# New priority keys for the list scheduler of an attention + gated-MLP kernel

## The chip, the cores and the metric

One core of a Trainium2 chip runs the whole kernel. The metric is device time in microseconds (us), the median of several executions.

## The reference, cut to what matters

```python
# B, H, S, D = 8, 12, 448, 64 ; float32 throughout
scores = cap * tanh((q @ k.T / 8) / cap)
attn   = exp(scores - max(scores)); attn /= sum(attn) + 1e-9
x      = heads_side_by_side(attn @ v)              # (8, 448, 768)
h      = relu(x @ w_in); u, w = h[..., :512], h[..., 512:]
w      = (w - mean(w)) / sqrt(var(w) + 1e-6)       # over the 512 features
gated  = u * (w_spatial @ w + b_spatial)           # mixes the 448 positions
out    = gated @ w_out                             # (8, 448, 768)
```

## The kernel before, in words

The Python code first lists every piece of work as a task (engine, modelled duration, a priority number called its key, the tasks it depends on, the buffers it takes). `Plan.order` then plays the engines forward in time with the modelled durations. Whenever an engine is free, it takes the task with the smallest key among those that are ready and whose buffers are free. The order that comes out is the order of the instructions on each engine's queue, and it is fixed: on the chip each queue runs in that order and waits for what it needs. Two rules matter beside the keys. A buffer of a kind is handed out strictly in the order of the keys of the tasks that ask for one, even when a later one is ready first. And TensorE (PE), which works either in the 64x64 tiles of the attention (mode "R") or with the whole 128x128 array (mode "N"), adds `STICK` to the key of a task that would change the mode.

**Attention** is done in 24 quads, three per batch; a quad (`quad_bnd`, number `turn`) is 4 heads. It loads the raw q and k of two head pairs (`raw`, 4 buffers) and v (`v`, 2 buffers: one quad's worth). Seven score groups of 8 matmuls (L594, `sc`) go to PSUM. ScalarE (ACT) takes the tanh of each (L598) into `tp` (6 buffers of two groups; a quad needs 4) and the exp of each pair (L605). Seven groups of 8 matmuls multiply by v (L615, `pv`). VectorE (DVE) folds the exps over keys to a maximum (`mx`), then to a sum (`sm`): six instructions each, L633 four times, L641, L643, in the single `red` buffer. For the quads 0 to 2 the sum is done on PE instead (L662, in the two `acc` PSUM buffers, brought out by ACT at L671). Small instructions make the denominators (`dn`, L652 to L685), which go through memory and come back spread over partitions (L686, L689). DVE multiplies (L698), and each head pair is cast (ACT, L355) and split (DVE, L351) into a high and a low part in an `xg` buffer (7 of them), the input of the MLP.

**The MLP** of a batch (`moe`) needs its three quads, as six `xg` chunks, and consists of 18 units on PE, each a chain of matmuls into one `acc` buffer: u (L754 to L756, 4 units of 18 matmuls), v (L776 to L781, 4 units, 66 matmuls in all), g (L845 to L850, 4 units of 11) and o (L870 to L872, 6 units of 12), 254 matmuls. In batch 0 the u units 0 and 1 come first, with 8 filler matmuls ahead (L753); in the others the four v units.

**The weights** arrive as 64-bit numbers: 12 pieces of w_in (`wi`), 12 of w_out (`wo`, through `xg` buffers), 4 of w_spatial (`ws`). A piece of `wi` or `wo` takes one POOL (GpSimd) instruction (L420), three on DVE (L424, L425, L427), a cast (ACT, L355) and a DVE subtraction (L351); `ws` has its subtraction on POOL.

The keys are sums: for stage `s` of quad `t`, index `i`, `4*t + BND_KEY[s] + BND_ADJ[s or "sc", t] + BND_KEY[s_]*i`; for unit `n` of batch `b`, `12*(b+1) + BND_KEY["moe"] + BND_ADJ["moe"b] + n*(span + span_b)/18`; the MLP's DVE and ACT tasks add `mv`; the weights have `BND_W_KEYS` and the `wi`, `ws`, `wo` entries.

Of the kernel before, what the change touches and what calls it, by code (L numbers as in the profile page):

```python
# [42 lines left out]
class Plan:  # L43
# [5 lines left out]
    SEM = {"T": 230.0, "V": 200.0, "A": 200.0, "P": 230.0, "S": 0.0}  # L49
    SAME = {"T": 0.0, "A": 60.0, "V": 60.0, "P": 60.0, "S": 0.0}  # L50
    HAND, WINDOW = 70.0, 4096 / 1.2
    TURN, STICK = 180.0, 5.6142

    OWN = {"vtr", "red3", "max", "stat", "gmul", "vadd", "xadd", "rec", "ones", "evl", "evh", "nb"}

# [160 lines left out]
def gpc(n):  # L216
# [26 lines left out]
CAP_BITS = 0x42200000  # L243
ANY_KEY = dict(moe=0.5, span=12.0, mv=0.0)
ANY_W_KEYS = 2, 0.5, 8, 9, 1, 5, 0.5
BND_KEY = dict(ld=20.2062, vld=16.3748, sc=-4.4101, th=2.6266, ex=-12.5751, pv=3.8334, sm=4.9568, mx=1.2536,
               dn=-1.9573, ev=0.5509, x=0.5743, moe=3.5126, span=11.5964, step=-1.1271, mv=-7.699, vld_=0.5863, sc_=0.1716,
               th_=0.234, ex_=3.1048, pv_=-0.3915, sm_=-0.1418, mx_=1.5249)
BND_ADJ = dict(sc0=-1.9208, sc1=-0.6751, sc2=-0.5665, sc3=0.6591, sc4=1.0022, sc5=0.9243, sc6=0.5641, sc7=3.5286,
               sc8=4.1291, sc9=2.1364, sc10=0.4432, sc11=-0.3562, sc21=1.0782, sc22=-2.0787, sc23=-1.8651, mx0=7.5468, mx1=4.1712,  # L250
               mx2=0.2306, mx3=-3.4986, mx4=-4.2501, mx5=-7.8699, mx6=-6.59, mx7=-4.2274, mx8=-1.6152, mx9=-1.0965, mx10=-2.503,
               mx11=2.4712, mx21=3.6487, mx22=7.5152, mx23=10.1101, sm0=-23.9232, sm1=-5.9121, sm2=-19.3382, sm3=-4.1068,
               sm4=-7.6692, sm5=-6.9113, sm6=-7.6076, sm7=-2.9296, sm8=-4.8786, sm9=-2.9017, sm10=0.1476, sm11=-1.028,
               sm21=7.8004, sm22=5.003, sm23=9.0892, dn0=-13.9326, dn1=2.5665, dn2=1.5054, dn3=3.678, dn4=5.4586, dn5=2.0101,
               dn6=-0.9345, dn7=1.341, dn8=5.2032, dn9=5.9753, dn10=6.5428, dn11=-0.3824, dn21=0.2627, dn22=-7.9155, dn23=32.9005,
               x0=-1.8155, x1=-12.9607, x2=-3.0392, x3=-3.3476, x4=1.7459, x5=0.4945, x6=3.9029, x7=6.1809, x8=0.3782, x9=6.0115,
               x10=5.0057, x11=0.7894, x21=7.5672, x22=-1.7504, x23=1.6104, moe0=-2.1731, moe1=4.7513, moe2=2.8101, moe3=2.4916,
               moe7=9.0071, span0=-2.667, span1=-3.3859, span2=-2.449, span3=-5.6885, span7=28.8127, mv0=4.9503, mv1=-2.4788,
               mv2=2.6326, mv3=3.2084, mv7=-12.8989, wi0=-3.2806, wi1=-21.6066, wi2=-37.6263, wi3=14.5167, wi4=16.5614,
               wi5=1.1376, wi6=13.0344, wi7=2.468, wi8=-18.9783, wi9=3.3202, wi10=-13.2504, wi11=-12.154, ws0=-12.654,  # L260
               ws1=-7.9959, ws2=-33.2129, ws3=-10.2049, wo0=-6.4452, wo1=-0.8201, wo2=2.6051, wo3=8.6589)
BND_V_FIRST = 1
WARM, WARM_N, FILL = 14, 512, 8
BND_W_KEYS = -14.6272, 0.1578, -3.1507, 14.803, -4.1788, 0.5729, 0.2535
SPARE = ()
PE_SUMS = 3
E_W = "PAV"
# [6 lines left out]
def attn_moe(ctx, tc, bounded, shared, qk, v, qk2, v2, cap, w_in, w_sp, w_out, out):  # L274
    nc = tc.nc
    TAGS, PTAGS = (BND_TAGS, BND_PTAGS) if bounded else (ANY_TAGS, ANY_PTAGS)
    KEY, W_KEYS, V_FIRST = (BND_KEY, BND_W_KEYS, BND_V_FIRST) if bounded else (ANY_KEY, ANY_W_KEYS, B)
    PS = bass.MemoryType.PSUM
# [159 lines left out]

    adj = lambda name, i: BND_ADJ.get(name + str(i), 0.0) if bounded else 0.0
    wi32, wo32 = w_in.bitcast(U32), w_out.bitcast(U32)  # L440
# [124 lines left out]
    def quad_bnd(b, n):  # L565

        at, turn = b * H + 4 * n, b * (NP // 2) + n
        own_key = lambda name: KEY[name] + BND_ADJ.get((name if name in ("mx", "sm", "dn", "x") else "sc") + str(turn), 0.0)
        kk = lambda name, i=0: at + own_key(name) + KEY.get(name + "_", KEY["step"]) * i
# [161 lines left out]
    def moe(b, xs):  # L731
        own_key = lambda name: KEY[name] + (BND_ADJ.get(name + str(b), 0.0) if bounded else 0.0)
        k0 = (b + 1) * H + own_key("moe")
# [221 lines left out]
```

## Time and profile before

| | |
|---|---|
| median of 3 runs | 729.02 us (728.62 to 729.78) |
| profiled execution, first to last instruction | 726.5 us |
| around the span (difference to the median) | 2.5 us |
| busy in the span | PE 713.2, DVE 600.4, ACT 479.9, POOL 78.4 us |
| matmuls | 4910 |
| granted TensorE clock, mean | 0.997 |

The profiled execution has no other time of its own than its span; the runs' median stands 2.5 us above it. Busy shares are averages over stages with different limits; a busy PE can still lose time between matmuls, since their ends are modelled.

### The profile page before, as it was taken

The numbers are of one execution on the slowest core, as the hardware profiler recorded it, in microseconds if no ns is written. First come the engines' busy times: TensorE is split into PE (matmuls) and PEld (weight loads), VectorE is DVE, ScalarE is ACT, GpSimd is POOL, SyncE is SP. The second block draws the span as 40 slices with busy tenths as digits, with TensorE's granted clock in tenths as the row PEclk, the third lists the DMA queues.
The fourth block names the chain that finished last, engine by engine and source line by source line (L and its number), as shares of the span: only waits on it lengthen the run. The fifth ranks groups of instructions, "written<-read, shape, count | busy, mean of one in ns | idle before, by whom it ended". The sixth has DMA issues, their size and how long they took to land.

```text
span 726.5 us, 12274 instructions
## 1 busy us (share of the span) xinstructions
PE 713.2 (98%) x4910; PEld 487.7 (67%) x4910; DVE 600.4 (83%) x849; ACT 479.9 (66%) x648; POOL 78.4 (11%) x71
## 2 busy tenths in 40 slices
PE   8998999999999999999999999999999999999997
PEld 3333576575668657785568688568566865699896
DVE  4899999999999989948999996299799778983520
ACT  6999757849883894649875833786876678424321
POOL 1234310600110001000120001000021000200100
PEclk9999999999999999999999999999999999999999
DMA  8564314524221431033321430124321131202002
GB/s 279 165 204 148 129 38 134 168 80 142 85 78 30 149 129 49 28 91 114 102 76 28 153 103 27 49 66 141 102 77 41 47 131 39 53 2 101 1 1 80
DMA packets 34263, 66.50 MB, mean 92 GB/s; under 512 B 6034, under 2 KB 21908, under 8 KB 34196
## 3 DMA queue, kind: packets, MB, share of 16 engines
q1 hardware_dynamic: 34196, 65.62, 28.3%
q8 instruction: 40, 0.66, 0.4%
q14 instruction: 27, 0.22, 0.1%
HBM read 54.40 MB, written 11.18 MB: 90 GB/s over the span
## 4 chain that ended last, share of the span: by engine, by line
PE 79%; DVE 12%; issue 4%; ACT 2%; DMA 1%; SPq 1%; POOL 0%; DVEq 0%; ACTq 0%; POOLq 0%
PE ps_s L594 13%; PE ps_x L615 13%; PE ps_acc L870 5%; PE ps_acc L871 5%; PE ps_acc L872 5%; PE ps_acc L754 4%; PE ps_acc L756 4%; PE ps_acc L755 4%; DVE red L633 4%; PE ps_acc L779 4%; PE ps_acc L780 3%; PE ps_acc L781 3%; PE ps_acc L848 2%; PE ps_acc L850 2%; PE ps_acc L849 2%
## 5 line engine op out<-in xcount | busy, mean ns | idle before, releaser
L598 ACT ACTIVATE tp<-ps_s,capt 128x896 f32<-128x896 f32 x168 | 162.2, 1003 | 28.6 <-PE ps_s L594 18.1
L633 DVE TENSOR_TENSOR red<-red,tp 128x1792 f32<-128x1792 f32 x90 | 140.9, 1566 | 22.5 <-ACT tp L605 20.8
L605 ACT ACTIVATE tp<-tp,capt 128x1792 f32<-128x1792 f32 (+1 forms) x96 | 154.0, 1606 | 1.5
L594 PE MATMUL ps_s<-raw 64*64 64x448 f32 x1344 | 147.1, 545 | 3.6 <-ACT tp L598 3.5
L615 PE MATMUL ps_x<-tp,v 64*64 64x448 f32 x1344 | 140.0, 536 | 0.5 <-ACT tp L605 0.4
L633 DVE TENSOR_TENSOR red<-tp 128x1792 f32<-128x1792 f32 x45 | 91.2, 2027 | 13.9 <-ACT tp L605 13.0
L615 PEld LDWEIGHTS ps_x<-tp,v 64*64 64x64 f32 x1344 | 51.3, 133 | 75.7 <-issue 68.2
L594 PEld LDWEIGHTS ps_s<-raw 64*64 64x64 f32 x1344 | 47.1, 132 | 80.1 <-issue 46.5
L803 POOL TENSOR_TENSOR lst<-lst,capt 128x1 f32<-128x1 f32 x32 | 34.9, 1091 | 526.7 <-DVE lst L801 482.9
L754 PE MATMUL ps_acc<-xg,wi_h 128*128 128x448 f32 x180 | 66.2, 368 | 0.5 <-ACT xg L355 0.5
L755 PE MATMUL ps_acc<-xg,wi_h 128*128 128x448 f32 x180 | 65.3, 363 | 0.7 <-DVE xg L351 0.6
L756 PE MATMUL ps_acc<-xg,wi_l 128*128 128x448 f32 x180 | 65.2, 362 | 0.0
L870 PE MATMUL ps_acc<-xg,wo_h 128*128 128x448 f32 x176 | 64.5, 367 | 0.0
L871 PE MATMUL ps_acc<-xg,wo_h 128*128 128x448 f32 x176 | 63.7, 362 | 0.6 <-DVE xg L351 0.6
L872 PE MATMUL ps_acc<-xg,wo_l 128*128 128x448 f32 x176 | 63.8, 362 | 0.0
L355 ACT CAST xg<-o 128x448 fp32r<-128x448 f32 x32 | 18.1, 566 | 55.0 <-DVE o L855 49.5
L641 DVE STREAM_TRANSPOSE red<-red 128x896 f32<-128x896 f32 x45 | 49.6, 1102 | 0.7
L779 PE MATMUL ps_acc<-wi_h,xg 128*128 128x512 f32 x126 | 50.1, 398 | 0.0
L643 DVE TENSOR_REDUCE st<-red 128x28 f32<-128x896 f32 x45 | 48.6, 1079 | 0.7
L780 PE MATMUL ps_acc<-wi_l,xg 128*128 128x512 f32 x126 | 49.1, 390 | 0.0
L781 PE MATMUL ps_acc<-wi_h,xg 128*128 128x512 f32 x126 | 49.1, 390 | 0.0
L633 DVE TENSOR_TENSOR red<-red 128x896 f32<-128x896 f32 x45 | 48.6, 1079 | 0.6
(146 smaller groups left out, 1110.1 us busy)
## 6 DMA issues: line engine op xcount, KB each, us to landing
raw<-in_qk SPq DMA_DIRECT2D x48, 448.0 KB
rr<-rd SPq DMA_DIRECT2D x48, 224.0 KB
out<-o SPq DMA_DIRECT2D x48, 224.0 KB
w<-in_w_in SPq DMA_DIRECT2D x12, 512.0 KB
v<-in_v SPq DMA_DIRECT2D x24, 256.0 KB
v<-in_v SPq DMA_DIRECT2D x24, 192.0 KB
xg<-in_w_out SPq DMA_DIRECT2D x12, 256.0 KB
rd<-dt SPq DMA_DIRECT2D x48, 3.5 KB
```

What stands on the lines that cost most here:

```text
L594: nc.tensor.matmul(ps.t[c * D:(c + 1) * D, e, :S], lhsT=f(raw[c].t)[r, k:k + D], rhs=f(raw[c].t)[r, :S], start=True, stop=True)
L598: th = add("A", act(PW, 1), kk("th", i), lambda ps=ps, tp=tp, o=o: nc.scalar.activation(out=tp.t[:, o:o + PW].rearrange("p (e q) -> p e q" ...
L605: ex = add("A", act_s(w, 1), kk("ex", i), lambda tp=tp, w=w: nc.scalar.activation(out=tp.t[:, :w], in_=tp.t[:, :w], func=AF.Exp, scale=ca) ...
L615: nc.tensor.matmul(x.t[e * D:(e + 1) * D, c, :S], lhsT=vts[g // 2].t[c * D:(c + 1) * D, (4 * (g % 2) + 2 * j + e) * D:(4 * (g % 2) + 2 * j ...
L633: nc.vector.tensor_tensor(o_(), i0(), i1(), op=op)
L754: nc.tensor.matmul(ps, lhsT=wi1_h[:, c, fs], rhs=x[:, XH:], start=(c == 0), stop=False)
L755: nc.tensor.matmul(ps, lhsT=wi1_h[:, c, fs], rhs=x[:, :S], start=False, stop=False)
L756: nc.tensor.matmul(ps, lhsT=wi1_l[:, c, fs], rhs=x[:, XH:], start=False, stop=(c == NP - 1))
L779: nc.tensor.matmul(ps, lhsT=x[:, XH:][:, ts], rhs=wi2_h[:, c], start=(c == 0), stop=False)
L870: nc.tensor.matmul(ps, lhsT=wo_h[:, c, ns], rhs=g[:, XH:], start=(c == 0), stop=False)
L871: nc.tensor.matmul(ps, lhsT=wo_h[:, c, ns], rhs=g[:, :S], start=False, stop=False)
L872: nc.tensor.matmul(ps, lhsT=wo_l[:, c, ns], rhs=g[:, XH:], start=False, stop=(c == 3))
```

## The change

Only numbers change: the keys of the stages (`BND_KEY`), their corrections per quad, batch and weight piece (`BND_ADJ`, which now has an entry for every quad and batch), the base keys of the weights (`BND_W_KEYS`), and `STICK`, from 5.6 to 11.6. Every task, instruction, buffer and byte stays; the order on the queues of PE, DVE, ACT, POOL and SP is computed from the new numbers.

```diff
-    TURN, STICK = 180.0, 5.6142
+    TURN, STICK = 180.0, 11.5841
...
-BND_KEY = dict(ld=20.2062, vld=16.3748, sc=-4.4101, th=2.6266, ex=-12.5751, pv=3.8334, sm=4.9568, mx=1.2536,
-               dn=-1.9573, ev=0.5509, x=0.5743, moe=3.5126, span=11.5964, step=-1.1271, mv=-7.699, vld_=0.5863, sc_=0.1716,
-               th_=0.234, ex_=3.1048, pv_=-0.3915, sm_=-0.1418, mx_=1.5249)
...
+BND_KEY = dict(ld=-23.2446, vld=64.3643, sc=-9.3854, th=15.363, ex=-45.84, pv=6.3869, sm=5.8599, mx=4.9369, dn=2.3698,
+               ev=-0.5327, x=-6.2772, moe=6.1778, span=13.9485, step=0.225, mv=-4.7549, vld_=1.3185, sc_=0.2564, th_=0.1728,
+               ex_=17.2099, pv_=-0.2428, sm_=24.2721, mx_=14.1049)
...
-BND_W_KEYS = -14.6272, 0.1578, -3.1507, 14.803, -4.1788, 0.5729, 0.2535
+BND_W_KEYS = -25.523, 4.0178, 8.8276, -2.372, -4.936, 32.4763, -6.7862
```

The keys of some tasks by the formulas above, before and after:

```
                                            before            after
cast of the first chunk, quad 0 / quad 1    -1.2 / -8.4       -55.0 / -42.8
max fold of quad 0, first to sixth step     8.8 to 16.4       -13.3 to 57.2
sum fold of quad 12, first to sixth step    53.0 to 52.2      58.9 to 180.3
chunk of quad 12 (x)                        48.6              53.9
MLP of batch 0, first and last unit         13.3, 21.8        8.7, 9.2
wi pieces of the v half, chunks 0 / 5       13.6 / -10.3      36.5 / 52.4
loads of quad 1: raw / of quad 0: v         23.5 / 14.5       -40.6 / 33.8
last quad (23): scores / v product          85.7 / 93.6       92.7 / 108.2
MLP of batch 6, first unit, step            87.5, 0.64        99.7, 0.68
```

## Rows read from the trace of the kernel before

**Rows 1.** The page's first line, the whole span

```profile
span 726.5 us, 12274 instructions
```

**Rows 2.** Windows by stage: us from A to B, busy us of each engine, clock

```profile
0.00:62.80 62.80, 59.78 (x570) 22.61 (x574) 49.38 (x70) 55.00 (x59) 22.29 (x25) 1.00 0.64 210
62.80:78.40 15.60, 11.44 (x56) 6.97 (x48) 15.02 (x26) 14.71 (x24) 2.54 (x3) 0.89 0.46 158
78.40:162.70 84.30, 83.25 (x575) 55.07 (x574) 83.09 (x140) 55.55 (x79) 21.31 (x17) 1.00 0.33 104
162.70:634.50 471.80, 471.80 (x3291) 323.55 (x3290) 414.11 (x551) 328.70 (x435) 29.60 (x24) 1.00 0.26 82
634.50:721.40 86.90, 86.90 (x428) 79.47 (x424) 38.83 (x66) 25.45 (x51) 2.66 (x5) 1.00 0.10 36
721.40:726.50 5.10, 0.02 (x1) 0.00 (x0) 0.00 (x0) 0.53 (x1) 0.00 (x0) 0.96 0.16 55
```

**Rows 3.** Timeline of PE around one attention stretch: start, us, line, count

```profile
257.46 0.40 PE L781 MATMUL ps_acc<-wi_h,xg 128*128 128x512 f32 x1
257.79 1.73 PE L594 MATMUL ps_s<-raw 64*64 64x448 f32 x16
259.34 1.68 PE L615 MATMUL ps_x<-tp,v 64*64 64x448 f32 x16
260.85 1.68 PE L594 MATMUL ps_s<-raw 64*64 64x448 f32 x16
...
267.61 0.93 PE L615 MATMUL ps_x<-tp,v 64*64 64x448 f32 x8
268.47 0.50 PE L779 MATMUL ps_acc<-wi_h,xg 128*128 128x512 f32 x1
268.81 0.39 PE L780 MATMUL ps_acc<-wi_l,xg 128*128 128x512 f32 x1
269.04 0.39 PE L781 MATMUL ps_acc<-wi_h,xg 128*128 128x512 f32 x1
```

**Rows 4.** Timeline of PE, starts of the first and last attention stretch

```profile
6.77 1.73 PE L594 MATMUL ps_s<-raw 64*64 64x448 f32 x16
...
628.35 0.98 PE L594 MATMUL ps_s<-raw 64*64 64x448 f32 x8
629.15 5.44 PE L615 MATMUL ps_x<-tp,v 64*64 64x448 f32 x56
```

**Rows 5.** Timeline of PE, start of the first MLP

```profile
66.29 2.62 PE L594 MATMUL ps_s<-raw 64*64 64x448 f32 x16 [2.89 <-ACT tp L598]
...
72.10 0.47 PE L754 MATMUL ps_acc<-xg,wi_h 128*128 128x448 f32 x1 [0.52 <-ACT xg L355]
...
89.49 0.40 PE L779 MATMUL ps_acc<-wi_h,xg 128*128 128x512 f32 x1
```

**Rows 6.** Timeline of DVE, chunks and weights of the first MLP, last chunks

```profile
45.73 0.61 DVE L698 TENSOR_TENSOR xf<-xf,rr 128x448 f32<-128x448 f32 x1
...
70.85 1.16 DVE L351 TENSOR_TENSOR xg<-xf,xg 128x448 fp32r<-128x448 f32 x2 [0.58 <-ACT xg L355]
...
87.56 0.68 DVE L351 TENSOR_TENSOR wi_l<-wy,wi_h 128x512 fp32r<-128x512 f32 x1
...
658.03 1.16 DVE L698 TENSOR_TENSOR xf<-xf,rr 128x448 f32<-128x448 f32 x2 [0.49 <-ACT xf L621]
```

**Rows 7.** Timeline of ACT, the sums of quad 2 leave PSUM

```profile
64.67 0.53 ACT L671 COPY u<-ps_acc 128x448 f32<-128x448 f32 x1
```

**Rows 8.** Timeline of POOL, one w_spatial piece, one w_in piece

```profile
51.29 9.14 POOL L351 TENSOR_TENSOR ws_l<-wy,ws_h 128x448 fp32r<-128x448 f32 x1 [3.24 <-DVE ws_h L382]
...
72.88 0.78 POOL L420 TENSOR_SCALAR wy<-w 128x512 f32<-128x512 f32 x1 [9.60 <-DMA w<-in_w_in]
```

**Rows 9.** Timeline of SP's DMA issues at the start

```profile
6.28 1.11 SPq L583 DMA_DIRECT2D v<-in_v  x2
7.58 1.15 SPq L576 DMA_DIRECT2D raw<-in_qk  x2
```

More of the change, by code (lines that the diff above doesn't have):

```diff
@@ L245 @@
 ANY_W_KEYS = 2, 0.5, 8, 9, 1, 5, 0.5
-BND_KEY = dict(ld=20.2062, vld=16.3748, sc=-4.4101, th=2.6266, ex=-12.5751, pv=3.8334, sm=4.9568, mx=1.2536,
-               dn=-1.9573, ev=0.5509, x=0.5743, moe=3.5126, span=11.5964, step=-1.1271, mv=-7.699, vld_=0.5863, sc_=0.1716,
-               th_=0.234, ex_=3.1048, pv_=-0.3915, sm_=-0.1418, mx_=1.5249)
[L249 to L261, printed above, removed]
@@ new lines @@
+BND_KEY = dict(ld=-23.2446, vld=64.3643, sc=-9.3854, th=15.363, ex=-45.84, pv=6.3869, sm=5.8599, mx=4.9369, dn=2.3698,
+               ev=-0.5327, x=-6.2772, moe=6.1778, span=13.9485, step=0.225, mv=-4.7549, vld_=1.3185, sc_=0.2564, th_=0.1728,
+               ex_=17.2099, pv_=-0.2428, sm_=24.2721, mx_=14.1049)
+BND_ADJ = dict(sc0=-30.5667, sc1=-21.3621, sc2=-17.1335, sc3=-8.3756, sc4=-4.9393, sc5=4.2055, sc6=2.7434, sc7=-0.2474,
+               sc8=0.4985, sc9=-1.9043, sc10=1.0047, sc11=-0.3935, sc12=-2.2382, sc13=-2.8258, sc14=-2.2096, sc15=-1.3068,
+               sc16=-3.7818, sc17=-4.3823, sc18=-5.4592, sc19=-5.2044, sc20=-2.3054, sc21=0.1061, sc22=9.7492, sc23=10.0707,
+               mx0=-18.2389, mx1=-18.752, mx2=-17.4529, mx3=-5.7358, mx4=-3.1789, mx5=-2.1209, mx6=-2.541, mx7=-4.9259,
+               mx8=-1.16, mx9=-0.9664, mx10=-1.4319, mx11=2.0044, mx12=3.2931, mx13=2.3977, mx14=0.4582, mx15=-0.3008,
+               mx16=-2.651, mx17=-5.2359, mx18=-2.5337, mx19=-3.3278, mx20=-3.1737, mx21=3.9766, mx22=14.3556, mx23=16.3248,
+               sm0=-86.6641, sm1=-10.5589, sm2=-1.174, sm3=-5.2213, sm4=0.0917, sm5=0.3787, sm6=-2.2041, sm7=-1.919, sm8=1.7682,
+               sm9=0.5525, sm10=0.1748, sm11=4.5405, sm12=5.0865, sm13=1.8553, sm14=2.3084, sm15=0.0565, sm16=-2.4687,
+               sm17=-3.9729, sm18=-1.8837, sm19=-2.3412, sm20=3.7351, sm21=4.7661, sm22=14.5067, sm23=35.9335, dn0=-39.7358,
+               dn1=-3.237, dn2=-2.8194, dn3=-6.128, dn4=-8.2448, dn5=-10.3257, dn6=-12.5898, dn7=-11.5319, dn8=-12.8005,
+               dn9=-16.7061, dn10=-20.7322, dn11=-10.6462, dn12=-0.4003, dn13=-15.9434, dn14=2.7064, dn15=11.5489, dn16=6.3924,
+               dn17=5.7939, dn18=10.0177, dn19=9.8358, dn20=12.3477, dn21=23.6499, dn22=56.7351, dn23=38.2856, x0=-48.7285,
+               x1=-40.5342, x2=-31.8316, x3=-12.6926, x4=-11.2882, x5=-11.1569, x6=-7.7226, x7=1.2989, x8=-3.7308, x9=3.7178,
+               x10=5.9412, x11=11.3293, x12=12.1362, x13=10.5414, x14=9.2954, x15=14.0304, x16=20.8839, x17=15.3991, x18=25.0656,
+               x19=19.8285, x20=26.636, x21=36.6564, x22=40.6067, x23=54.2646, moe0=-9.4513, moe1=3.1367, moe2=-1.9137,
+               moe3=-3.9354, moe4=-2.6612, moe5=-1.0644, moe6=9.5145, moe7=8.6224, span0=-13.4158, span1=-8.6342, span2=-11.9909,
+               span3=-9.604, span4=-7.5288, span5=-3.3905, span6=-1.6881, span7=5.4694, mv0=-12.0547, mv1=-10.6373, mv2=-0.513,
+               mv3=4.9073, mv4=10.5984, mv5=13.6555, mv6=5.8573, mv7=33.1423, wi0=-32.5096, wi1=-47.8424, wi2=-65.1659,
+               wi3=5.2602, wi4=12.8733, wi5=-18.1684, wi6=4.0051, wi7=-5.5585, wi8=-66.0527, wi9=-12.3347, wi10=-37.5645,
+               wi11=53.8635, ws0=-24.258, ws1=-32.0782, ws2=-98.6782, ws3=-11.5562, wo0=-7.583, wo1=-1.6578, wo2=-15.1862,
+               wo3=8.9802)
```

## The prediction, made before the changed kernel was seen

> **What bounds the kernel now.** The first line gives the span, 726.5 us [rows 1]; the windows by stage say where PE stands still in it [rows 2]. From 162.7 to 721.4 us it never does: 471.80 busy of 471.80, then 86.90 of 86.90. Its idle time is 62.80 - 59.78 = 3.0 us in the first window, 15.60 - 11.44 = 4.2 in the second, 1.0 in the third and 5.1 behind the last matmul, where the last output is copied and stored. An order of issue can thus give time only in three places: the first 163 us, the price of each change between 64x64 tiles and the full array, which a busy PE hides, and a stall that is not there yet.
>
> The price of a mode change comes from the timeline of PE [rows 3]. Entering the attention, the step from the last MLP matmul to the first score is 257.79 - 257.46 = 0.33 us against 0.23 (269.04 - 268.81) between two MLP matmuls, and the first 16 matmuls take 259.34 - 257.79 = 1.55 against 260.85 - 259.34 = 1.51: 0.14 us together. Leaving it, the last 8 take 268.47 - 267.61 = 0.86 against 1.51/2 = 0.75, and the first MLP step is 268.81 - 268.47 = 0.34 against 0.23: 0.22 us. A visit of the attention mode so costs 0.36 us. The timeline of PE has 26 of them, the first at 6.77 and the last at 628.35 [rows 4]: 9.4 us in all.
>
> The dearest single place is the hand-over to the first MLP, 62.8 to 78.4 us. PE did there 16 score matmuls (1.5 us), 8 fillers and 24 matmuls of u (32 x 0.20 = 6.4 us, by 86.9/428 in the last long window [rows 2]), with the end of an earlier group some 8.4 us of work in 15.6. [...]
>
> **The change, part by part.** No instruction, byte or buffer is added, so every duration stays; what moves is order.
>
> *Hand-over.* Buffers of `xg` are handed out by key. Before, quad 1's chunks (-8.4) stand ahead of quad 0's (-1.2). Quad 0 was multiplied at 45.73 but had to wait for quad 1, whose split ran at 70.85 [rows 6], and the first real matmul of the MLP came at 72.10 [rows 5]. After, quad 0 is first (-55.0 against -42.8), so its two chunks are there some 20 us early. The MLP also needs an `acc` buffer, which the sums of quad 2 leave at 64.67 + 0.53 = 65.20 [rows 7]. From 65.20 the 8 fillers and the 12 matmuls of chunks 0 and 1 in two units take 4.0 us, and the waiting scores 1.5. Quad 1's chunks are split by 70.85 + 1.16 = 72.0 as before; its 12 matmuls then end at 72.0 + 2.4 = 74.4 instead of 78.4. That is 3.9 us gained. Bounds: nothing, if another queue is late there (ACT, whose shift, copies and tanh stand in one line), and the whole 7.2 us. I take 3.9, since the quads' own pace is not changed by this key.
>
> *STICK.* It doubles, while quads stay 4 and batches 12 apart in key. A visit serves one quad as a rule, since `tp` holds one and a half and DVE must fold before more scores fit; 21 quads follow the first three, so some 22 visits are the least, and 26 can go up by a few if the new keys break quads. Bounds: 4 fewer, -1.4 us, to 4 more, +1.4. I take 3 fewer, -1.1 us: a larger `STICK` leaves fewer short returns.
>
> *First loads.* At the start v of quad 0 was issued at 6.28 and raw of quad 1 at 7.58 [rows 9]; the new keys (33.8 and -40.6) swap them, so v comes after 896 KB more, at the 210 GB/s of the first window [rows 2] 4.4 us later. The first v product can wait for that while ACT goes on with the tanhs and PE has the sums (L662) to do. Bounds 0 (hidden) and +4.4 (all of it on PE); I take +1.0, because PE idles little in that stretch and has other groups ready.
>
> *Folds last.* The later steps of the folds move behind almost everything on DVE: 57.2 instead of 16.4 for quad 0, 180.3 instead of 52.2 for quad 12. So denominators, chunks and MLP steps overtake them. The scheduler leaves DVE no free time while a task is ready, so the same work is done by the same time, in another order. I put this at nothing: after 162.7 us DVE is busy 414.11 of 471.80 and PE has MLP backlog at every moment [rows 2]. If that cover goes, a fold step late costs PE what the step costs, some 2 us each time. A gain beyond the hand-over is excluded there, since PE has no idle time left to give back.
>
> *Weights.* Their order among themselves changes, and the v half's chunks 0 and 5 now stand among the fold steps (36.5, 52.4) instead of before them. Nothing in the sum; the price if it goes wrong is the second rival.
>
> Sum: 726.5 - 3.9 - 1.1 + 1.0 = 722.5 us of span. With the 2.5 us that the median of the runs stands above the profiled span this is **725.0 us**, 0.55% less.
>
> **Rivals.**
>
> *No change (729.0 us).* DVE bounds the start: it is busy 15.02 of 15.60 and 83.09 of 84.30 us between 62.8 and 162.7 [rows 2], so PE cannot get its quads sooner, and 4 us won at the hand-over are lost again in a later wait for `tp`. For it: DVE's full windows. Against it: as soon as the first MLP runs, PE has 254 matmuls, some 51 us, that ask little of DVE.
>
> *Last weight pieces late (733 to 737 us).* Before, the last w_in piece ended at 87.56 + 0.68 = 88.2 and the first v unit began at 89.49 [rows 5, 6]: no slack. After, two pieces come in the midst of the folds. A POOL instruction for such a piece took 0.78 us at 72.88, but one of the same engine beside DVE's folds took 9.14 at 51.29 [rows 8]. One piece stretched from 0.78 to 4.9, half way, costs 4.1 us, and to 9.14, 8.4 us; this decides if PE has no attention group ready then. For it: no slack before. Against it: after the first steps of a fold the new keys still let any piece that has landed go ahead of the later steps.
> [...]
>
> *A stall ahead of the last MLP (732 us).* The last quad's chunks were multiplied at 658.03 + 1.16 = 659.2, 24.6 us after its v products ended at 634.6 [rows 4, 6]; the rest of batch 6, 170 matmuls or 34 us, covered that. After, scores of quad 23 break into the MLP of batch 6 once its key passes 92.7 + 11.6 = 104.3, after 7 units (99.7 + 0.68 n), with 141 matmuls or 28.4 us left: enough by 3 us with 1 us for cast and split. If the return comes for the last score group (94.2 + 11.6 = 105.8), 9 units are done, 112 matmuls or 22.5 us are left, and PE waits 24.6 + 1.0 - 22.5 = 3.1 us. It decides when the cover falls under 25.6 us. Against it: DVE is less than half busy in the last window.
>
> **How the numbers follow.** The forecast has a chance of 0.55 (its own range 720 to 727.5: the whole hand-over and 4 visits fewer give 726.5 - 7.2 - 1.4 + 2.5 = 720.4; at 727.5 it ends where no difference begins). No change has 0.20, late weights 0.15, the late stall 0.10. A measurement of this kernel can tell some 0.2%, 1.5 us, from no change. Faster: 0.55; same: 0.20; slower: 0.25. The range reaches from 719.5 to 735.0; the upper half of the late weights (0.07) and small tails stay outside.
>
> **What would show it.** In the profile of the changed kernel: the first real L754 near 66 us, and the window up to the end of the first 24 u matmuls shorter by some 4 us; 22 to 24 visits of the attention on PE; the first L615 at 14 to 17 us; PE without idle time from some 160 us to the last matmul; quad 23's chunks split before batch 6's last o unit ends. I am wrong if PE idles after 160 us, if the first v units start later than 90 us, if the visits grow in number, or if ACT or SP hold PE at the hand-over in a new way.

## The result: 0.54% slower

The changed kernel takes **733.07 us** (median of 5 runs, 732.21 to 733.76) against 729.02 us for the kernel before in the same comparison: a ratio of **1.0054, 95% interval 1.0041 to 1.0066**. The forecast was 725.0 us. The time lies inside the range, on the wrong side of no change.

The first lines of the page of the changed kernel, then the same line of the kernel before:

```profile
span 731.3 us, 12268 instructions
PE 714.2 (98%) x4910; PEld 485.4 (66%) x4910; DVE 601.7 (82%) x849; ACT 479.0 (65%) x648; POOL 56.3 (8%) x71
```

```profile
PE 713.2 (98%) x4910; PEld 487.7 (67%) x4910; DVE 600.4 (83%) x849; ACT 479.9 (66%) x648; POOL 78.4 (11%) x71
```

Of the 4.8 us that the span grew, PE was busy 1.0 us longer, so it stood still 3.8 us longer. The windows of the changed kernel by the same stages as [rows 2] (length, then busy us of PE, PEld, DVE, ACT, POOL, then clock) say where. The first MLP now begins at 67.95 us, the end of its hand-over is at 84.48, the next attention follows its last matmul at 161.08, and the closing stretch without attention starts at 650.82:

```profile
0.00:62.80 62.80, 57.86 (x546) 21.54 (x550) 50.55 (x71) 53.97 (x62) 17.50 (x25) 1.00 0.62 206
...
62.80:67.95 5.15, 5.15 (x57) 1.74 (x49) 5.12 (x10) 4.13 (x7) 0.00 (x0) 1.00 0.52 141
...
67.95:84.48 16.53, 16.53 (x132) 9.13 (x128) 14.07 (x23) 15.36 (x21) 3.95 (x3) 1.00 0.61 189
84.48:161.08 76.60, 71.18 (x443) 49.60 (x439) 75.84 (x129) 49.70 (x73) 12.79 (x16) 1.00 0.32 102
161.08:650.82 489.74, 488.16 (x3381) 334.84 (x3380) 422.07 (x557) 332.32 (x439) 19.55 (x24) 1.00 0.25 78
650.82:726.10 75.28, 75.28 (x370) 68.55 (x366) 34.05 (x64) 22.97 (x49) 2.51 (x4) 1.00 0.14 47
```

PE's idle time, window minus busy, before [rows 2] and after: the start 3.0 and 4.9; the hand-over 4.2 and **0**; the rest of the first MLP 1.0 and **5.4**; the long middle 0 and **1.6**; behind the last matmul 5.1 and 5.2. That is +1.9 - 4.2 + 4.4 + 1.6 + 0.1 = +3.8. The hand-over's idle time is gone, as forecast, and 4.4 us more are idle again before 161 us.

Idle time alone doesn't place the loss, because the two ends of the first MLP aren't the same work. Up to 161.08 us the changed kernel has done 336 products with v, the kernel before up to 162.70 us 368. The 32 that are still to come take 32 x 0.094 = 3.0 us (1.51/16, [rows 3]). So on equal work the changed kernel is 161.1 + 3.0 - 162.7 = **1.4 us** behind at the end of the first MLP. From there to the last matmul it takes 565.0 us against 558.7, which is **3.3 us** more beyond these 32, and 0.1 us are lost at the end.

The attention mode has 31 visits (stretches in PE's timeline) instead of 26. All five more lie ahead of 161 us; behind it both kernels have 21. Ahead of 161 us PE is busy 0.7 us less on equal work, although five visits more cost some 5 x 0.36 = 1.8: in the hand-over the clock is 1.00 now, and at 0.89 over 15.6 us, 11% of them, up to 1.7 us had been lost. Behind 161 us, 1.6 of the 3.3 us are idle time, and 1.7 are time in which the profile calls PE busy, with no visit more. Part of that are short waits which the modelled ends of the matmuls cover. Here 16 products take 1.89 us to the next matmul and 8 take 1.03, instead of 1.51 and 0.75 [rows 3]; over all visits behind 161 us such steps add up to 1.3 us more than before:

```profile
427.03 1.68 PE L623 MATMUL ps_x<-tp,v 64*64 64x448 f32 x16
428.92 1.88 PE L602 MATMUL ps_s<-raw 64*64 64x448 f32 x16 [0.21 <-ACT tp L606]
...
435.13 0.93 PE L623 MATMUL ps_x<-tp,v 64*64 64x448 f32 x8
436.16 0.98 PE L602 MATMUL ps_s<-raw 64*64 64x448 f32 x8
```

The hand-over in PE's timeline: no idle time, the first real matmul at 69.67 instead of 72.10 [rows 5], and the last of the first 24 u matmuls at 81.03, behind attention visits that now stand between them:

```profile
64.80 3.22 PE L623 MATMUL ps_x<-tp,v 64*64 64x448 f32 x32
67.95 1.89 PE L761 MATMUL ps_acc<-wi_h 128*128 128x448 f32 x8
69.67 0.37 PE L762 MATMUL ps_acc<-xg,wi_h 128*128 128x448 f32 x1
...
81.03 0.36 PE L764 MATMUL ps_acc<-xg,wi_l 128*128 128x448 f32 x1
```

The waits of PE in the changed kernel (us in total, times, longest):

```profile
PE ps_s L602 <- ACT tp L606: 4.1, 7, 1.6
PE ps_acc L856 <- DVE o L863: 1.9, 1, 1.9
PE ps_acc L670 <- ACT tp L613: 1.6, 2, 0.9
PE wps L918 <- DVE capt L921: 1.2, 1, 1.2
PE ps_acc L787 <- ACT o L363: 1.1, 1, 1.1
```

The new ones are scores that wait for a tanh (7 places instead of 3), a g unit that waits for DVE at 122.0 us, and a v unit that waits at 250.4 us for `o` to be evacuated.

### The profile page after: what moved, and what is told of

It is laid out like the page before. It is cut to its first block, busy times and chain, and to the rows that moved or that the text cites. A ratio compares the mean times of both kernels' runs of the same rounds, so it can differ in the third digit from the quotient of the medians.

```text
span 731.3 us, 12268 instructions
## 1 busy us (share of the span) xinstructions
PE 714.2 (98%) x4910; PEld 485.4 (66%) x4910; DVE 601.7 (82%) x849; ACT 479.0 (65%) x648; POOL 56.3 (8%) x71
## 4 chain that ended last, share of the span: by engine, by line
PE 74%; ACT 10%; DVE 10%; DMA 2%; issue 2%; SPq 0%; POOL 0%; DVEq 0%; ACTq 0%; POOLq 0%
PE ps_s L602 11%; PE ps_x L623 11%; ACT tp L606 4%; PE ps_acc L762 4%; PE ps_acc L878 4%; DVE red L641 4%; PE ps_acc L764 4%; PE ps_acc L763 4%; PE ps_acc L787 4%; PE ps_acc L880 4%; PE ps_acc L879 4%; PE ps_acc L788 4%; PE ps_acc L789 4%; ACT tp L613 4%; PE ps_acc L856 2%
## 5 line engine op out<-in xcount | busy, mean ns | idle before, releaser
L623 PE MATMUL ps_x<-tp,v 64*64 64x448 f32 x1344 | 140.1, 537 | 0.9 <-ACT tp L613 0.9
L623 PEld LDWEIGHTS ps_x<-tp,v 64*64 64x64 f32 x1344 | 50.7, 133 | 75.9 <-issue 71.4
L811 POOL TENSOR_TENSOR lst<-lst,capt 128x1 f32<-128x1 f32 x32 | 26.1, 817 | 537.7 <-DVE lst L809 470.0
L641 DVE TENSOR_TENSOR red<-red 128x896 f32<-128x896 f32 x45 | 50.3, 1118 | 0.6
```

Source lines behind the costliest of these rows:

```text
L623: nc.tensor.matmul(x.t[e * D:(e + 1) * D, c, :S], lhsT=vts[g // 2].t[c * D:(c + 1) * D, (4 * (g % 2) + 2 * j + e) * D:(4 * (g % 2) + 2 * j ...
L641: nc.vector.tensor_tensor(o_(), i0(), i1(), op=op)
```

## The experiments

Below, "after" is the changed kernel at 733.07 us; each ratio is to the kernel before as it ran in the same comparison, on the same chip. The kernel before took 728.50 to 729.58 us (medians) in these comparisons, so runs of different ones are set side by side by their ratios: 0.001 is 0.7 us.

### Is the hand-over worth what it gives?

One key changed back, so that quad 1's chunks come first as before (e6):

```diff
-               x0=-48.7285, x1=-40.5342,
+               x0=-33.7228, x1=-40.5342,
```

> The changed kernel with one part undone: quad 1's chunks are keyed before quad 0's again, so the hand-over to the first MLP is laid out as in the kernel before (one N stretch of 8 units at 62.7 us in the scheduler's own order, then 8 score groups), 29 visits. Theory A (the hand-over is worth the 3.9 us that it gave, and what is lost behind it comes from other keys): 733.1 + 3.9 - 2 x 0.36 = 736.3, a ratio of 1.010. Rival B (DVE is full until about 161 us in either order, so what the hand-over gives is taken back before 161 us): 733 or less, a ratio of at most 1.0055, with a later hand-over and fewer stalls between 84 and 161 us.

Measured **733.35 us**, 1.0073 [1.0059, 1.0087]. That lies between theory A (1.010) and rival B (at most 1.0055), and neither bound is met. The time is after's within 0.3 us, but the kernel before took 728.50 us in this comparison, and by the ratios e6 is 1.4 us slower than after, with intervals that overlap. What rival B said of the trace came: a later hand-over and fewer stalls behind it. The windows of e6 (it has the first MLP at 73.52 us, and the long stretch behind it at 88.65):

```profile
0.00:67.95 67.95, 59.60 (x570) 22.32 (x574) 55.20 (x78) 56.26 (x63) 20.62 (x25) 0.99 0.61 202
67.95:88.65 20.70, 19.67 (x144) 10.03 (x137) 19.18 (x31) 18.37 (x29) 2.67 (x3) 0.86 0.43 140
88.65:161.27 72.62, 71.61 (x458) 50.30 (x454) 71.86 (x124) 48.00 (x70) 14.58 (x15) 1.00 0.35 111
```

The idle time of PE up to the end of the first MLP is 8.35 + 1.03 + 1.01 = 10.4 us here and 4.94 + 5.42 = 10.4 in after: the same sum, only earlier. The attention that follows the first MLP begins within 0.2 us of the same moment, first after, then e6:

```profile
161.08 0.98 PE L602 MATMUL ps_s<-raw 64*64 64x448 f32 x8
```

```profile
161.27 0.98 PE L582 MATMUL ps_s<-raw 64*64 64x448 f32 x8
```

Up to these two rows both have done the same number of matmuls of each kind. So the hand-over is worth 0.2 us by the profiles and 1.4 by the ratios, not 3.9. (e6 has two visits fewer ahead of 161 us; at 0.36 us each that could hide another 0.7.) DVE is busy 75.84 of 76.60 us there in after and 71.86 of 72.62 in e6. Whether that full DVE is the cause was tried by taking work from it. The middle steps of a weight piece were left out, first for w_out alone (e3, e4), then for all 24 pieces in after, in e6 and in the kernel before (e13 to e15, the same edit without `late`):

```diff
         for i, (e, d, fn) in enumerate(ops):
+            if late and i in (2, 3):
+                fn = lambda: None
```

> The changed kernel without the two middle steps of DVE (L433 and L435) on each of the 12 pieces of w_out, which leaves out part of the conversion of w_out: 24 instructions of 0.41 us, 9.8 us of DVE, between 85 and 160 us. Theory A (DVE, through the pieces of w_out and the casts behind them, sets the pace of the first MLP, and there the 3.9 us won at the hand-over are lost): the 6.1 us that PE loses over its visits between 84 and 161 us shrink to 3 or less, 3 us or more off the time, 730 or less, a ratio of at most 1.0013. Rival B (the stalls there come from the order on ACT and on PE, not from DVE's load): less than 1 us off, 732 to 733, a ratio of 1.004 to 1.0055.

> The kernel before with the same two steps of DVE (its L425 and L427) left out for the 12 pieces of w_out, so again a part of the conversion of w_out is missing. Theory A (DVE's load sets the pace of the first MLP): the kernel before lost only 2.5 us between 87 and 163 us over its visits, so at most 2.5 us less, 726.5, a ratio of 0.9966, clearly less than what the same edit takes off the changed kernel. Rival B (DVE's load is nowhere on the path): 729 +- 0.5, a ratio of 1.

e3: **730.63 us**, 1.0018 [1.0009, 1.0027]. e4: **727.09 us**, 0.9973 [0.9962, 0.9985]. Both kernels gain some 2 us (2.4 and 1.95). DVE's load is on the path in either order, but it is not what sets them apart: theory A wanted 3 us or more in after and clearly less in the kernel before, and rival B less than 1 us or nothing.

> The changed kernel without the two middle steps of DVE (L433 and L435) on all 24 pieces of w_in and w_out, which leaves out part of the conversion of both: 24 instructions of 0.68 us and 24 of 0.43 us, 26 us less for DVE before 161 us. Theory A (DVE's load before 161 us takes back what the hand-over gives): at least 5 us less than the changed kernel, 728 or less, and at least 2 us less than the same kernel with quad 1's chunks first (the next run). Rival B (the order of what is issued behind 84 us takes it back): 730 or more, and within 0.7 us of the next run.

> The run with quad 1's chunks keyed first (733.35 us with all of DVE's work) without the same two steps. Theory A: DVE's relief alone, without the hand-over's gain, so 2 to 4 us above the run before this one. Rival B: within 0.7 us of it.

> The kernel before without the same two steps of DVE on all 24 pieces: 26 us less for DVE before 163 us. It loses 16.4 us of PE time before 163 us beyond its warm-up's and its visits' own price. Theory A (DVE is what PE waits for there, at the rate of the run without w_out's steps): 26/9.8 x 1.95 = 5.2 us less, 724, a ratio of 0.993. Rival B (latencies and ACT hold PE there as well): 2 to 3 us less, 726.5, a ratio of 0.9965. What it keeps ahead of the changed kernel with the same relief is what the keys behind the hand-over cost without DVE.

e13: **728.69 us**, 0.9998 [0.9989, 1.0006]. e14: **730.88 us**, 1.0033 [1.002, 1.0045]. e15: **725.92 us**, 0.9961 [0.9949, 0.9973]. With 26 us less on DVE the two hand-overs are 2.2 us apart (2.5 by the ratios) instead of 0.3 (1.4). The row that began at 161.08 and 161.27 us shows it in e13 and then in e14:

```profile
157.06 0.61 PE L604 MATMUL ps_s<-raw 64*64 64x448 f32 x4
```

```profile
159.63 0.61 PE L584 MATMUL ps_s<-raw 64*64 64x448 f32 x4
```

They are now 2.6 us apart instead of 0.2. Of theory A's two bounds one is met (2.2 us apart, for at least 2) and one is missed (728.69, for 728 or less). By the profiles DVE's load takes most of the hand-over's gain back; the times alone, 1.4 and 2.5 us apart, each give or take more than 1 us, only agree with it. It isn't all of it: of 26 us taken from DVE only 4.4, 2.5 and 3.1 us reach the time (4.1, 2.9 and 2.8 by the ratios). In the kernel before that is about rival B's 2 to 3 us, not theory A's 5.2. And e13 still has 2.98 us of idle time in 84 to 161 us:

```profile
84.00:161.00 77.00, 74.02 (x481) 51.11 (x485) 70.51 (x108) 51.91 (x74) 13.22 (x15) 1.00 0.32 105
```

Scores that wait for a tanh are PE's longest wait in e13 (3.3 us in 4 places). DVE is still busy 70.51 of 77.00 us there, so this run doesn't say what the chain from score to tanh to the next score would cost without DVE.

### What is a visit worth?

In the kernel before, the first MLP unit behind a visit was moved into the middle of that visit at ten places, all other engines as they were (e9):

```diff
 PE's order, ten times:
-  16 matmuls L594, 16 L615, ... , then MLP unit, MLP unit, ...
+  half of the visit, MLP unit, other half, then MLP unit, ...
```

> The kernel before with its order written out and, at ten places between 191 and 473 us of the scheduler's order, the first unit of the MLP stretch that follows moved into the middle of the attention visit ahead of it: 36 visits instead of 26, nothing else moved on any engine. Theory A (the prediction's step: a visit costs its two mode changes, 0.36 us, and PE has no idle time to hide it in): 10 x 0.36 = 3.6 us more, 732.6, a ratio of 1.005. Rival B (the price of a visit is hidden): 729 +- 0.5, a ratio of 1. Rival C (a later second half of a visit delays scores, tanh and folds as well): 735 or more, a ratio of at least 1.008.

Measured **733.41 us**, 1.0053 [1.0039, 1.0068], 3.8 us for ten visits: theory A, 0.38 us each (0.28 to 0.50 by the interval). PE stays busy throughout, so the price is mode changes alone; the window from 162 to 634 us:

```profile
162.00:634.00 472.00, 471.86 (x3245) 320.78 (x3247) 410.89 (x542) 326.84 (x433) 29.57 (x23) 1.00 0.26 81
```

The reverse in after: four lone score groups moved on PE into the next visit, 27 visits (e2).

> The changed kernel with its order written out, and four lone score groups, each of which was a visit of the attention mode by itself, moved on PE into the visit that follows: 27 visits instead of 31. Theory A (a visit costs what its two mode changes cost, 0.36 us, and nothing hides it): 4 x 0.36 = 1.4 us less, 731.6, a ratio of 1.0036 to the kernel before. Rival B (the price of a visit is hidden, or the later scores bring a wait for tanh as long): no change, 733.1 +- 0.4, or up to 1 us more.

Measured **737.13 us**, 1.0111 [1.0096, 1.0126]: 4 us more, not 1.4 less. Neither theory had that. Two of the four moves brought new waits. Most of the loss falls at one of them: the visit at 202.53 us begins 1.1 us later than in after (201.39), the next one 4.5 us later (236.16 against 231.61). There the group's tanh and exp moved with it on ACT. The two merges at 145 to 150 us cost nothing in the profile (e2 is 1.5 us behind after in the visit ahead of them and 0.7 in the visit that follows). PE's timeline in the worse place:

```profile
202.53 1.73 PE L605 MATMUL ps_s<-raw 64*64 64x448 f32 x16
204.67 0.98 PE L605 MATMUL ps_s<-raw 64*64 64x448 f32 x8 [0.40 <-ACT tp L609]
205.47 3.19 PE L626 MATMUL ps_x<-tp,v 64*64 64x448 f32 x32
209.17 1.88 PE L605 MATMUL ps_s<-raw 64*64 64x448 f32 x16 [0.51 <-ACT tp L609]
```

In after the tanhs and the exp behind the lone score group at 189.83 us ran on ACT from 191.46 to 195.21 us, under MLP matmuls; the next visit came at 201.39. Sent with the others in e2, PE meets the third group while two PSUM buffers still wait for ACT, and stands 0.40 us there and 0.51 us at 209.17. At this place the short visit, which keeps ACT fed, is the cheaper way.

The new keys with the old `STICK` (e5):

```diff
-    TURN, STICK = 180.0, 11.5841
+    TURN, STICK = 180.0, 5.6142
```

> The changed kernel with STICK at its old 5.6142 and every new key kept: the list scheduler then lays out 57 visits of the attention mode instead of 31. Theory A (a visit costs its two mode changes, 0.36 us, and nothing more): 26 x 0.36 = 9.4 us more than the changed kernel, 742.5, a ratio of 1.0185. Rival B (a visit is mostly hidden by other waits): 733 to 735. Rival C (the price of broken quads is that scores, tanh and folds come later, on top of the mode changes): 748 or more, a ratio above 1.026.

Measured **748.78 us**, 1.0278 [1.0262, 1.0294], rival C. 26 more visits at e9's 0.38 us would be 9.9 of the 15.7 us (16.3 by the ratios); most of the rest is idle time of PE behind 161 us, 1.37 + 5.31 = 6.7 us instead of 1.6:

```profile
161.00:300.00 139.00, 137.63 (x904) 90.93 (x903) 129.47 (x177) 94.62 (x130) 5.17 (x8) 1.00 0.25 79
300.00:650.00 350.00, 344.69 (x2383) 224.39 (x2385) 286.92 (x366) 233.78 (x304) 20.12 (x14) 1.00 0.24 77
```

### The stall at 250 us

In after PE waits for an evacuation of `o` that stands behind a chunk cast on ACT; e1 exchanges the two:

```diff
 ACT's order near 250 us:
-  CAST xg<-xf, COPY o<-ps_acc
+  COPY o<-ps_acc, CAST xg<-xf
```

> The changed kernel with its whole order of issue written out, and one pair of instructions on ACT exchanged: the evacuation of `o` at 250.91 us goes ahead of the chunk cast at 250.44, which waited 2.13 us for DVE while PE, waiting for the evacuation, stood 1.26 us. Theory A (PE has work at every moment after 161 us, so each stall of PE there is lost for good): about 1.2 us less than the changed kernel, 731.8, a ratio of 1.0038 to the kernel before; the wait of L787 for L363 goes from PE's list of waits. Rival B (another engine sets the pace of that stretch and takes the time back): within 0.4 us of 733.1, a ratio of 1.0055, with another stall of PE of about 1 us behind 251 us.

Measured **732.74 us**, 1.0047 [1.0034, 1.006]: 0.3 us, within what can be told from nothing. ACT's timeline, after and then e1:

```profile
250.44 0.57 ACT L363 CAST xg<-xf 128x448 fp32r<-128x448 f32 x1 [2.13 <-DVE xf L706]
250.91 0.53 ACT L363 COPY o<-ps_acc 128x448 f32<-128x448 f32 x1
```

```profile
250.90 0.53 ACT L366 COPY o<-ps_acc 128x448 f32<-128x448 f32 x1 [1.95 <-DMA out<-o]
```

Ahead of the cast the copy waits for its buffer `o`, which an output store still reads: a second wait lay hidden under the first. In e1 the copy comes 2.48 us behind the copy before it (248.42 us); in after that one began at 247.78, so the exchange could bring 250.91 - 247.78 - 2.48 = 0.65 us, not 1.2, and of that 0.3 at most is seen.

### Could the order or another engine be mended?

The new start with the old order behind it, and the reverse (tasks keyed by their start ranks in the two orders):

```diff
+    if bounded:
+        plan.STICK = 0.0
+        for t in plan.tasks:
+            t.key = ORDER[t.seq]
```

> New order in the first 84 us (start-up and hand-over of the changed kernel), order of the kernel before for the rest, by the tasks' start ranks in the two orders, STICK as before; 36 visits. Theory A (the new start and hand-over are worth 3.9 us and the loss comes from the new keys behind them): 729.0 - 3.9 + 10 x 0.36 = 728.7, a ratio of 1.0. Rival B (DVE takes the gain back in the first MLP whatever the order behind it): 729 + 3.6 = 732.6 or more, a ratio of at least 1.005.

> The reverse: order of the kernel before in the first 84 us, new order for the rest, by start ranks; 32 visits. Theory A (the loss sits in the new keys behind the hand-over, 8 us of it): 729.0 + 8 = 737 or more, a ratio of at least 1.011. Rival B (what is behind the hand-over only takes back what the hand-over gave): 729 + 6 x 0.36 = 731.2, a ratio of 1.003.

(The edit set `STICK` to 0 in both, not "as before": the ranks alone make the order.) e7: **737.43 us**, 1.0122 [1.0106, 1.0137]. e8: **741.43 us**, 1.0181 [1.0167, 1.0195]. Both are slower than either parent and say nothing for the theories: each got stalls that neither parent has, 3.6 us for a DMA of v in e7 and 5.1 us for an `xf` on ACT in e8. The two orders can't be joined at 84 us by their ranks.

One cost in the scheduler, the bias rows, set near what the chip takes (3.1 us on DVE in after, from 53.88 us; e12):

```diff
-            l.append(add("V", 1500, key, parts, [a], [y]))
+            l.append(add("V", 3300, key, parts, [a], [y]))
```

> The changed kernel with one number of the scheduler's costs set to what the chip takes: the parse of the bias rows on DVE, reckoned with 1.5 us, took 3.1 us at 53.88 us; the scheduler is told 3.3. 48 of 980 places on PE, 4 on DVE, 26 on ACT and 18 on SP change. Theory A (the new order is laid out just in time for the scheduler's costs, and the stalls come where the chip is later than they say): 1 to 2 us less than the changed kernel, 731 to 732, a ratio of 1.003 to 1.004. Rival B (that cost is not what makes the order late): 733 +- 0.5, a ratio of 1.005 to 1.006.

Measured **733.31 us**, 1.0057 [1.0042, 1.0072]: rival B. Setting that cost right brings nothing.

The last subtraction of the weight pieces moved from DVE to POOL in the kernel before, for w_out (e10) and for all (e11):

```diff
-            (E_W[2], st2(E_W[2], n), lambda: sub(E_W[2], lo, yf(), f(hi))),
+            ("P", st2("V", n), lambda: sub("P", lo, yf(), f(hi))),
```

> The kernel before with its order written out and the last subtraction of the 12 w_out pieces moved from DVE (0.42 us each, 5.0 us in all) to POOL. Theory A (DVE's load before 163 us is on the path, by the 1.95 us that 9.8 us less of it gave): 5.0/9.8 x 1.95 = 1.0 us less, 728.0, a ratio of 0.9987. Rival B (POOL and DVE hold each other up by what the subtraction takes on POOL, 1.1 to 2.4 us): no gain, or up to 2 us more.

> The same for all 24 weight pieces, w_in's 12 (0.70 us each on DVE) too: 13.4 us off DVE before 163 us. Theory A: 13.4/9.8 x 1.95 = 2.7 us less, 726.3, a ratio of 0.9963. Rival B (POOL and DVE hold each other up, and POOL's next piece stands behind the subtraction): no gain or slower, 729 to 734, with longer folds on DVE beside POOL's instructions before 90 us.

e10: **731.81 us**, 1.0032 [1.0018, 1.0046]. e11: **734.34 us**, 1.007 [1.0055, 1.0085]. Both are slower, as rival B said, and by slightly more than its ranges. In e11 the same instruction of DVE, the multiply of a chunk, gets longer in half of its cases: up to 90 us three took 1.09 to 1.71 us and three 0.62. In the kernel before all six took 0.61 to 0.62. The kernel before and then e11 (ns min/median/max):

```profile
L698 DVE TENSOR_TENSOR xf<-xf,rr x6: 610/613/619, 45.7 to 85.4; 128x448 f32<-128x448 f32 x6
```

```profile
L701 DVE TENSOR_TENSOR xf<-xf,rr x6: 615/852/1711, 45.4 to 86.9; 128x448 f32<-128x448 f32 x6
```

Two of the longer ones, 2.72 us together, began at 45.35 us, while POOL did a subtraction and then the next pieces. DVE and then POOL in e11:

```profile
45.35 2.72 DVE L701 TENSOR_TENSOR xf<-xf,rr 128x448 f32<-128x448 f32 x2
```

```profile
45.16 1.42 POOL L354 TENSOR_TENSOR wi_l<-wy,wi_h 128x512 fp32r<-128x512 f32 x1 [6.66 <-ACT wi_h L358]
46.55 2.06 POOL L423 TENSOR_SCALAR wy<-w 128x512 f32<-128x512 f32 x2
```

POOL beside it was not always enough: in the kernel before the multiply at 46.87 us took 0.61 us, although a POOL instruction of 1.03 us began at 47.03. What makes the longer ones longer no run shows. Rival B named two causes, that POOL and DVE hold each other up and that POOL's next piece stands behind the subtraction; the two runs don't tell them apart. Both are a reason to take work off DVE by dropping it rather than by moving it to POOL.

Dropping one step alone, the one that adds the lowest three bits of the mantissa to a weight (e16):

```diff
+            if i == 3:
+                fn = lambda: None
```

> The kernel before without the one step of DVE (its L427) that adds the lowest three bits of the mantissa to the pieces of w_in and w_out, so the weights are cut to 21 bits: 12 instructions of 0.68 us and 12 of 0.43 us, 13 us less for DVE. Theory A: 13.3/9.8 x 1.95 = 2.6 us less, 726.4, a ratio of 0.9964, faster than both kernels. Rival B (what PE waits for there is not DVE's load): within 0.5 us of 729.

Measured **726.54 us**, 0.9962 [0.9949, 0.9975]: faster than the kernel before by 0.38%, and so than after, as theory A said, at the price of three bits in w_in and w_out.

## Why the prediction was wrong, step by step

**Hand-over (-3.9 us): the step that failed.** What it said of the place itself came in part: PE's idle time between the end of the attention and the first u units went from 4.2 us to nothing, and the clock there from 0.89 to 1.00. But the first real matmul came at 69.67 us, not near 66, and the first 24 u matmuls ended at 81.2 instead of 74.4, because attention visits were put between them. What failed is the sum, which let the 3.9 us stand to the end. The 7.2 us of its bounds are the window's 15.6 us less an estimate of 8.4 us of work: the window shows 4.2 us of them as idle time and up to 1.7 at a clock of 0.89 [rows 2], and no run shows the rest. The prediction's rule for gains ("An order of issue can thus give time only in three places") was applied to PE alone. From 20 to 160 us DVE is as full as PE (busy 135.6 and 132.9 us in after), and what PE gains ahead of DVE it waits for behind it. The rival "no change" had this mechanism, and e6 shows it with equal sums of idle time, 10.4 us in both: a first MLP that begins 5.6 us later (73.52 against 67.95) ends 0.2 us later. The argument against the rival (51 us of MLP matmuls that ask little of DVE) missed that the conversion of w_out and the folds of later quads fill DVE there (75.84 of 76.60 us from 84.48 us).

**Folds last (nothing): the second step that failed, by 3.3 us.** Behind the first MLP the changed kernel takes 3.3 us longer on equal work, with as many visits. "PE has MLP backlog at every moment" doesn't help a PE that takes its instructions in order: the v unit at 250 us waited 1.1 us while other MLP work stood behind it, for a copy that was held by a cast and, under that, by a store (e1). Some 1.3 us more are short waits inside the visits. e6, with the other hand-over, has this stretch as long (570.0 us to the end of its span against 570.2). So it comes from the order behind the hand-over; which keys make it, no run shows.

**STICK (-1.1 us): wrong sign of the number of visits.** The price of a visit was right, 0.36 us worked out, 0.38 measured in e9. Their number was wrong: 31, not 23, so at this price +1.8 us in place of -1.1. But e9's visits stand where PE is always busy, and the five more stand ahead of 161 us, where PE has idle time; no run took just these out. What was forecast from `STICK` alone depends on the keys it acts with: at its old value the new keys give 57 visits.

**First loads (+1.0 us): right in sign, too small.** The first L623 came at 18.99 us, later than the 14 to 17 forecast and 5.0 us behind that of the kernel before (14.02). PE idled 1.9 us more in the first 62.8 us.

**Weights, and the stall ahead of the last MLP:** neither came. The first v unit began at 87.89 us, 1.6 us earlier than before, and PE is busy 75.28 of the last 75.28 us.

That "every duration stays" didn't hold on POOL: the same instructions are busy 56.3 us there instead of 78.4.

So the 4.8 us of span are, by place and on equal work, 1.4 up to the end of the first MLP, 3.3 behind it and 0.1 at the end. Two of the prediction's signs of being wrong came: idle time behind 160 us, and more visits. Shown by runs: that the hand-over's gain doesn't last (e6), and the price of a visit where PE is always busy (e9). That DVE's load takes most of the gain back is what the profiles of e13 and e14 show, and their times agree. With 26 us off DVE ahead of 161 us the kernel before is still 2.8 us ahead of after (e15 against e13), which agrees with a loss that lies mostly behind. The cause of these 3.3 us is open: the exchange in e1 uncovered a second wait, and no run removed the waits in the visits. Open is also what share of the first MLP's remaining idle time comes from ACT's order and what share from the length of the chain from score to tanh to fold.

## What to carry to other kernels

Before counting a gain on the busiest engine, look at which other engine is full over the same stretch, and up to when: a stall removed early can come back as a stall later (10.4 us of idle time up to 161 us in after and in e6 alike), and the test is whether the next common milestone (here the end of the first MLP, on equal work) moves. Where PE changes modes, price each visit, but don't merge visits by count: a lone score group that starts a chain on ACT and DVE can pay for itself, as one of the four did here (e2, 737.13 us). In the stretch with two full engines only less work gave time (e16, 726.54 us), and moving work from DVE to POOL gave none (e10, 731.81 us, and e11, 734.34). And compare windows at equal work: a busy PE hid half of what was lost behind the first MLP (1.7 of 3.3 us).

## What was not expected of the hardware

- A DVE instruction of 0.61 us took up to 1.71 us in e11, where POOL has the subtractions, and the fold's 128x896 step of 1.07 us on average 1.56, while its first 128x1792 step stayed at 2.17 (2.15 before). One w_in subtraction took 1.87 us on average on POOL against 0.70 on DVE:

```profile
L354 POOL TENSOR_TENSOR wi_l<-wy,wi_h 128x512 fp32r<-128x512 f32 x12 | 22.3, 1867 | 31.0 <-ACT wi_h L358 31.0
```

- The granted clock differed around the same wait. In after and in e1 the g unit at 122 us waits 1.9 us for DVE; between 120 and 140 us the mean granted clock was 1.00 in after and 0.91 in e1, where PE's order up to there is the same:

```profile
120.00:140.00 20.00, 17.41 (x117) 11.74 (x109) 19.87 (x35) 10.25 (x18) 4.96 (x8) 1.00 0.48 154
```

```profile
120.00:140.00 20.00, 18.11 (x115) 13.12 (x109) 19.08 (x34) 9.37 (x16) 4.39 (x8) 0.91 0.48 155
```

  So single profiles can differ in the clock at the same place, and e1's verdict rests on the times of its runs and on where its copy stands.
